# C of all head pairs from unsplit float32 weights, in 64x32 array tiles, in a packed attention and two-MLP kernel

## The chip, the cores and the metric

The kernel runs on one core of a Trainium2 chip. The metric is the device time of one execution in microseconds (us); less is better. The engines are PE (TensorE, matrix products), DVE (VectorE), ACT (ScalarE) and POOL (GpSimd); SP is the queue that starts transfers. The trace also shows the clock that PE was granted, 1.00 for 2.4 GHz and 0.50 for 1.2 GHz.

## The reference

q, k and v have the shape [8 batches, 8 heads, 576, 64], p has [8, 8, 32, 64]; all is float32, and the weights arrive as float64.

```python
scale = 1.0 / np.sqrt(q.shape[-1])
def sm_attn(qq, kk, vv):
    s = scale * np.matmul(qq, kk.transpose(0, 1, 3, 2))
    a = np.exp(s - np.max(s, axis=-1, keepdims=True))
    return np.matmul(a / (np.sum(a, axis=-1, keepdims=True) + 1e-09), vv)
p_packed = sm_attn(p, k, v)                # 32 packed keys per head
out = sm_attn(q, p_packed, p_packed)       # [8, 8, 576, 64]
x = out.transpose(0, 2, 1, 3).reshape(4608, 512)
g = x @ w_gate                             # [512, 1536]
x = g * (1 / (1 + np.exp(-g))) * (x @ w_val) @ w_out
out = ((x @ w1) * (x @ w2)) @ w3 @ w_out2  # second MLP
```

## The kernel before

**Order of the work.** A prologue (to about 119 us), written out by hand as a schedule of half steps, makes P = p_packed for 16 units, one for each batch b and half Q of the heads (four heads of 32 packed keys, so P is 128 x 64). `pa_P` (L545) scales P, `pa_PT` (L565) transposes it on PE. The attention of the queries ends in aT, the 32 weights of each query for each head. Instead of multiplying aT by P and the result by w_gate and w_val, the kernel first makes C = P·W, which has only 32 rows for each head, and then aT·C. This is exact algebra: `c_mm` makes C, `stage1` (L676) multiplies by aT and applies the gate, `stage3` (L701) multiplies by w_out.

**The 48 steps.** The batches go in four pairs P (P = 0 to 3 in the loop `for n, (P, f) in enumerate(steps)`, L878), and the 1536 gate and value columns in 12 blocks f of 128 + 128. A step makes C of the next step, `stage1` of both batches of the pair, and half of the `stage3` of three earlier blocks. The steps fill 119 to 870 us. The second MLP (L975 on) fills the rest.

**Precision.** A product of two float32 numbers is made as three float32r matmuls of halves, high·high, high·low and low·high. The halves come from `split`: ACT rounds to the high half, DVE or POOL subtracts. A plain float32 matmul is exact without splitting; the trace shows two records for each.

**C before.** For pairs 1 to 3, `w_load` fetches W's block into a `vl` buffer with tag "wf", `w_split` halves it (ACT: wh, L92; POOL: wl, L88), and `c_mm` takes twelve 128x128 matmuls of 256 columns. The weights are PTh and PTl, the halves of P transposed, laid out so that two heads and both batches of a pair fill the 128 columns, with zeros (from `mask`) where a head meets the other's rows. Pair 0 uses `c_first`: eight float32 matmuls, 128 rows by 64 columns, two side by side, from W as it was converted. `c_out` moves C out of PSUM as halves ch (ACT) and cl (DVE), in one operation each for pair 0 and in three each for the others. `q_mm` (scores of the queries) takes PT, the sum of PTh and PTl (L161), with four 128x32 array tiles side by side.

**Names and queues.** pc is C in PSUM; psq and psp are scores of the queries and of p; pg and pv are the gate and the value product; px is stage3's; acc is its sum over blocks. The PSUM pool of the steps, `ps`, has four buffers of two banks. In the prologue and in the second MLP the order on each engine is the code's; in the steps between, a scheduler orders the instructions of ACT, DVE, POOL and SP. During pair 1, 16 pieces of w1 and w2 are converted (`w12_conv`): a load raw_w, a shift vx_w (DVE, L345), ACT's w12t (L342), two DVE operations (L352, L355) and a store w12d.

Of the kernel before, what the change touches and what calls it, by code (L numbers as in the profile page):

```python
# [38 lines left out]
def packed_attention_moe_kernel(  # L39
# [112 lines left out]
    def q_T(b, Q):  # L152
        t = q_t.pop((b, Q))
        qT = qp.tile([128, 2, S], F32, tag="qT", name=f"qT{b}_{Q}")
        for pr in range(2):
            nc.vector.transpose(out=qT[:, pr], in_=t[:, pr].rearrange("p n d -> p (n d)"))
        PT = qp.tile([128, 128], F32, tag="PT", name=f"PT{b}_{Q}")
        for e in range(2):
            cols = slice(64 * ((b + e) % 2), 64 * ((b + e) % 2) + 64)
            hi, lo = (x[:, 2 * Q + e, b // 2 - 1, cols].bitcast(F32) for x in (PTh, PTl))  # L160
            nc.vector.tensor_tensor(out=PT[:, 64 * e:64 * e + 64], in0=hi, in1=lo, op=ALU.add)  # L161
        qT_t[b, Q] = (qT, PT)

    PTd_t = {}
# [18 lines left out]
    def q_rmm(b, Q):  # L183
        qT, PTd = qT_t.pop((b, Q)), PTd_t.pop((b, Q))
        if Q == 0:
            sT_t[b] = qp.tile([128, 2, 2, HS], F32, tag="sT", name=f"sT{b}")
        t = psum(f"psq{b}_{Q}")
        for at in range(4):
            hq = (at + 2 * (b % 2)) % 4
            for e in range(2):  # L190
# [1 line left out]
                nc.tensor.matmul(
                    t[32 * at:32 * at + 32, e, 0:HS].rearrange("j (m p) -> j m p", m=NR // 2),
                    lhsT=PTd[es, hs[hq]], rhs=qT[es, :, hs[hq]],
                    start=True, stop=True, tile_position=(64 * e, 32 * at))
# [221 lines left out]
    def c_first(f):  # L417
        w = wf_t.pop((0, f))
        t = psum(f"pc0_{f}").rearrange("p b (q n) -> p b q n", q=2)
        for b in range(2):  # L420
            for Q in range(2):
                for e in (b, 1 - b):
                    at = 64 * (e ^ b)
# [4 lines left out]
        return t  # L428

    def c_mm(P, f):  # L430
        if P == 0:
            t = c_first(f)
            if C_t.get("later"):
                return C_t["later"].append((P, f, t))
            return c_out(P, f, t)
        wh, wl = W_t.pop((P, f))
        t = psum(f"pc{P}_{f}").rearrange("p a (k n) -> p (a k) n", k=2)
        for kt in range(4):
            for x, (a, w) in enumerate(((PTh, wh), (PTh, wl), (PTl, wh))):
                nc.tensor.matmul(t[:, kt], lhsT=a[:, kt, P - 1, :], rhs=w[:, kt],  # L440
                                 start=(x == 0), stop=(x == 2))
        c_out(P, f, t)

    def c_out(P, f, t):
        hi = cp.tile([128, 2, 2, 256], F32R, tag="ch", name=f"ch{P}_{f}")
# [1 line left out]
        if P == 0:
            nc.scalar.copy(hi, t)
            sub(lo, t, hi)
            C_t[P, f] = (hi, lo)  # L450
            return
        tv = t.rearrange("p (q e) n -> p e q n", e=2)
        nc.scalar.copy(hi[0:64], tv[0:64])
        for e in range(2):
            nc.scalar.copy(hi[64:128, 1 - e], tv[64:128, e])  # L455
        sub(lo[0:64], tv[0:64], hi[0:64])
        for e in range(2):
            sub(lo[64:128, 1 - e], tv[64:128, e], hi[64:128, 1 - e])
# [85 lines left out]
    def pa_P(u):  # L544
# [13 lines left out]
        P_t[u] = Pz
        if u < 4:
            Pd = pa.tile([128, 2, 64], F32, tag="Pd", name=f"Pd{u}")  # L560
            for e in range(2):
                nc.vector.tensor_scalar(Pd[:, e], t[:, 0:64], sm, None, op0=ALU.mult)
            Pd_t[u] = Pd

    def pa_PT(u):  # L565
        b, Q = divmod(u, 2)
        Pz = P_t.pop(u)
        tb = psum1(f"pPT{u}")
        t = tb[:, 0:128]
        nc.tensor.transpose(t, Pz.rearrange("p a b -> p (a b)"), ident)  # L570
        if u < 4:
            nc.tensor.transpose(tb[:, 128:256], Pd_t.pop(u).rearrange("p a b -> p (a b)"), ident)
            PTd = pa.tile([128, 128], F32, tag="PTd", name=f"PTd{u}", bufs=4)
            nc.scalar.copy(PTd, tb[:, 128:256])
            PTd_t[b, Q] = PTd
            nc.scalar.copy(PT0[:, 2 * Q:2 * Q + 2, b], t.rearrange("p (e j) -> p e j", e=2))
            return
        at = [(2 * Q + e, b // 2 - 1, slice(64 * ((b + e) % 2), 64 * ((b + e) % 2) + 64)) for e in range(2)]
        for e in range(2):
            nc.scalar.copy(PTh[(slice(0, 128),) + at[e]], t[:, 64 * e:64 * e + 64])  # L580
        for e in range(2):
            sub(PTl[(slice(0, 128),) + at[e]], t[:, 64 * e:64 * e + 64], PTh[(slice(0, 128),) + at[e]])
# [529 lines left out]
```

## Time and profile before

| | us |
|---|---|
| median of three runs | 1445.25 (1442.3 to 1448.73) |
| the profiled execution | 1441.93, its span 1440.2 |
| PE busy | 1393.1 (97%) |
| DVE busy | 780.2 (54%) |
| ACT busy | 642.5 (45%) |
| POOL busy | 457.7 (32%) |
| mean granted clock of PE | 0.983 |

The span is what lies between the first and the last instruction of the profiled execution. Busy times are sums over the span. PE's records overlap, since matmuls are pipelined, so the distance between starts is what counts there.

### The profile page before, as it was taken

What the parts mean: (1) busy time and instruction counts of PE and PEld (TensorE: products, weight loads), DVE (VectorE), ACT (ScalarE), POOL (GpSimd) and SP (SyncE); (2) the same over time, 40 slices, a digit from 0 to 9 for tenths busy, and PEclk for the clock granted to TensorE, in tenths of its full rate; (3) what the DMA queues carried; (4) which work ended last, traced back from release to release, by engine and by line L of the source; (5) the groups of instructions that cost most, each with busy time, mean ns of one, the idle gap of its engine ahead of it and who ended that gap; (6) DMA issues with size and microseconds to landing.
All of it is one profiled execution on the core that took longest, in us unless ns stands there. A gap on an engine that the chain in (4) does not pass through costs nothing. (4 is left out here: it accounts for less than half of the span.)

```text
span 1440.2 us, 25384 instructions
## 1 busy us (share of the span) xinstructions
PE 1393.1 (97%) x9960; PEld 1302.1 (90%) x9960; DVE 780.2 (54%) x1188; ACT 642.5 (45%) x1077; POOL 457.7 (32%) x341
## 2 busy tenths in 40 slices
PE   7679999999999999999999999999999999999998
PEld 5457998999999999999989999989989899899997
DVE  3467798767875455756366647962333413334130
ACT  5575545536655355564464433643323323233231
POOL 0334133434544434455243223721202112021120
PEclk9888999999999999999999999999999999999999
DMA  9997575676533322215353324964827548275451
GB/s 270 239 248 205 163 210 188 160 237 166 165 83 83 117 60 70 66 53 176 96 157 100 131 72 174 339 242 154 256 75 236 179 133 253 92 223 180 133 168 44
DMA packets 175255, 230.26 MB, mean 160 GB/s; under 512 B 69408, under 2 KB 102176, under 8 KB 175136
## 3 DMA queue, kind: packets, MB, share of 16 engines
q1 hardware_dynamic: 175136, 228.64, 52.2%
q8 instruction: 79, 1.29, 0.4%
q14 instruction: 40, 0.33, 0.1%
HBM read 179.04 MB, written 49.55 MB: 159 GB/s over the span
## 5 line engine op out<-in xcount | busy, mean ns | idle before, releaser
L88 POOL TENSOR_TENSOR ul<-u,uh 128x576 fp32r<-128x576 f32 x96 | 145.4, 1519 | 247.7 <-ACT uh L92 247.3
L1005 POOL TENSOR_TENSOR c<-s,s 128x384 f32<-128x384 f32 x48 | 48.8, 1016 | 376.0 <-ACT s L1000 375.6
L701 PE MATMUL px<-ul,woh 128*128 128x288 f32 x768 | 165.3, 297 | 1.3 <-POOL ul L88 1.3
L701 PE MATMUL px<-uh,woh 128*128 128x288 f32 x768 | 165.4, 297 | 0.7 <-ACT uh L92 0.7
L701 PE MATMUL px<-uh,wol 128*128 128x288 f32 x768 | 164.9, 296 | 0.0
L1000 ACT COPY s<-pA 128x384 f32<-128x384 f32 x144 | 69.0, 479 | 181.1 <-PE pA L985 181.1
L88 DVE TENSOR_TENSOR cl<-pc,ch 64x512 fp32r<-64x512 f32 (+2 forms) x120 | 105.1, 900 | 55.4 <-ACT ch L455 47.6
L701 PEld LDWEIGHTS px<-uh,woh 128*128 128x128 f32 x768 | 124.1, 189 | 2.4 <-issue 1.4
L701 PEld LDWEIGHTS px<-ul,woh 128*128 128x128 f32 x768 | 124.3, 190 | 1.5 <-POOL ul L88 1.5
L701 PEld LDWEIGHTS px<-uh,wol 128*128 128x128 f32 x768 | 124.3, 189 | 0.0
L88 POOL TENSOR_TENSOR wl<-wf,wh 128x1024 fp32r<-128x1024 f32 x36 | 86.9, 2414 | 97.4 <-ACT wh L92 86.7
L1049 PE MATMUL po<-wo_hi,abl 128*128 128x512 f32 x288 | 112.2, 389 | 0.0
L1049 PE MATMUL po<-wo_lo,abh 128*128 128x512 f32 x288 | 112.1, 389 | 0.0
L1049 PE MATMUL po<-wo_hi,abh 128*128 128x512 f32 x288 | 112.0, 389 | 0.0
L711 DVE TENSOR_TENSOR acc<-acc,px 128x576 f32<-128x576 f32 x96 | 71.2, 746 | 66.1 <-PE px L701 65.9
L92 ACT CAST uh<-u 128x576 fp32r<-128x576 f32 x96 | 64.6, 674 | 93.5 <-DVE u L683 93.1
L88 DVE TENSOR_TENSOR abl<-ab,abh 128x768 fp32r<-128x768 f32 x48 | 48.6, 1013 | 105.2 <-ACT abh L92 105.2
L683 DVE TENSOR_TENSOR u<-u,pv 128x576 f32<-128x576 f32 x96 | 72.1, 751 | 48.8 <-PE pv L676 43.2
L88 POOL TENSOR_TENSOR wol<-wof,woh 128x512 fp32r<-128x512 f32 x48 | 66.9, 1406 | 88.3 <-ACT woh L92 80.7
L676 PE MATMUL pg<-aTh,ch 128*128 128x288 f32 x384 | 85.2, 304 | 4.8 <-DVE acc L711 3.3
L681 ACT ACTIVATE u<-pg 128x576 f32<-128x576 f32 x96 | 62.5, 651 | 49.4 <-PE pg L676 46.6
L676 PE MATMUL pg<-aTl,ch 128*128 128x288 f32 x384 | 83.3, 299 | 0.0
(362 smaller groups left out, 3544.1 us busy)
## 6 DMA issues: line engine op xcount, KB each, us to landing
ws<-wsd SPq DMA_DIRECT2D x245, 256.0 KB, 3.1
wf<-Wd SPq DMA_DIRECT2D x36, 512.0 KB, 3.4
raw_w<-in_moe_w_dram SPq DMA_DIRECT2D x32, 512.0 KB, 4.5
wsd<-ws SPq DMA_DIRECT2D x49, 256.0 KB, 4.0
raw_wo<-in_moe_w_out_dram SPq DMA_DIRECT2D x20, 512.0 KB, 4.4
km<-in_k_dram SPq DMA_DIRECT2D x16, 576.0 KB, 8.0
vm<-in_v_dram SPq DMA_DIRECT2D x16, 576.0 KB, 8.0
wof<-wod SPq DMA_DIRECT2D x36, 256.0 KB, 2.8
```

The lines of the kernel that those rows point to most:

```text
L88: eng.tensor_tensor(out=out, in0=src, in1=hi.bitcast(F32), op=ALU.subtract)
L92: nc.scalar.copy(hi, src)
L676: nc.tensor.matmul(t[:, hf, 0:HS], lhsT=w[:, b % 2, Q, cols], rhs=x[:, Q, hf, :], start=first, stop=last,)
L681: nc.scalar.activation(u, t[:, :, 0:HS], AF.Silu)
L683: nc.vector.tensor_tensor(out=u, in0=u, in1=t[:, :, 0:HS], op=ALU.mult)
L701: nc.tensor.matmul(t[:, hf, 0:HS], lhsT=w[:, 128 * d:128 * d + 128], rhs=x[:, hf, :], start=first, stop=last,)
L711: nc.vector.tensor_tensor(out=o, in0=o, in1=t[:, :, 0:HS], op=ALU.add)
L1000: nc.scalar.copy(o, t)
L1005: on.tensor_tensor(out=r, in0=o, in1=t, op=op)
L1049: nc.tensor.matmul(t, lhsT=a[:, j, cols], rhs=w[:, f], start=first, stop=last)
```

## The change

P is kept once, transposed, as PTd [128, 16 units, 128] in float32, doubled over the two halves of the partitions. C of all pairs is made by one `c_mm` from W as float32: sixteen matmuls, each with one head of one batch (64 rows) against its 256 columns, into 32 columns of the array; eight such tiles (two row halves by four column quarters) stand side by side. `w_split`, `c_first`, the masked Pz, PTh, PTl and PT0 go; `c_out` is one ACT and one DVE operation for all pairs. The order of the heads becomes `at ^ (b % 2)`. `q_mm` and `q_rmm` read PTd, with 64x32 tiles. `w_load` now fills the `wgv` buffers (tags "wh" and "wl" in turn, four in all) that held the halves.

```diff
-    PTh = pt_pool.tile([128, 4, NPR - 1, 128], F32R, name="PTh")
-    PTl = pt_pool.tile([128, 4, NPR - 1, 128], F32R, name="PTl")
-    PT0 = pt_pool.tile([128, 4, 2, 64], F32, name="PT0")
-    mask = const.tile([128, 2, 64], F32, name="mask")
+    PTd = pt_pool.tile([128, 2 * B, 128], F32, name="PTd")
...
+    def head(b, at):
+        return at ^ (b % 2)
...
     def q_mm(b, Q):
...
         for hf in range(2):
             for at in range(4):
-                hq = (at + 2 * (b % 2)) % 4
+                hq = head(b, at)
+                es = slice(64 * (hq % 2), 64 * (hq % 2) + 64)
                 nc.tensor.matmul(
-                    t[32 * at:32 * at + 32, hf, 0:HS],
-                    lhsT=PT[:, 32 * hq:32 * hq + 32],
-                    rhs=qT[:, hq // 2, HS * hf:HS * hf + HS],
-                    start=True, stop=True, tile_position=(0, 32 * at),
+                    t[hs[at], hf, 0:HS],
+                    lhsT=PTd[es, 2 * b + Q, hs[hq]],
+                    rhs=qT[es, hq // 2, HS * hf:HS * hf + HS],
+                    start=True, stop=True, tile_position=(64 * (hq % 2), 32 * at),
                 )
...
     def w_load(P, f):
-        t = vl.tile([128, 4, 2, 128], F32, tag="wf", name=f"wf{P}_{f}")
+        t = wgv.tile([128, 4, 2, 128], F32, tag=("wh", "wl")[f % 2], name=f"wf{P}_{f}")
...
+    def c_mm(P, f):
+        w = wf_t.pop((P, f))
+        t = psum(f"pc{P}_{f}").rearrange("p b (q n) -> p b q n", q=2)
+        for Q in range(2):
+            for at in range(4):
+                for b in range(2):
+                    hq = head(b, at)
+                    es = slice(64 * (hq % 2), 64 * (hq % 2) + 64)
                     nc.tensor.matmul(
-                        t[at:at + 64, b, Q], lhsT=PT0[:, 2 * Q + e, b],
-                        rhs=w[:, 2 * Q + e].rearrange("p g n -> p (g n)"),
-                        start=True, stop=True, tile_position=(0, at))
+                        t[hs[at], b, Q], lhsT=PTd[es, 2 * (2 * P + b) + Q, hs[hq]],
+                        rhs=w[es, 2 * Q + hq // 2].rearrange("p g n -> p (g n)"),
+                        start=True, stop=True, tile_position=(64 * (hq % 2), 32 * at))
...
-        Pz = pa.tile([128, 2, 64], F32, tag="Pz", name=f"Pz{u}")
-        for e in range(2):
-            nc.vector.scalar_tensor_tensor(
-                Pz[:, e], t[:, 0:64], sm, mask[:, e], op0=ALU.mult, op1=ALU.mult)
+        Pd = pa.tile([128, 2, 64], F32, tag="Pd", name=f"Pd{u}")
+        nc.vector.tensor_scalar(
+            Pd, t[:, 0:64].rearrange("p (o d) -> p o d", o=1).to_broadcast([128, 2, 64]), sm, None, op0=ALU.mult)
...
+        t = psum1(f"pPT{u}")[:, 0:128]
+        nc.tensor.transpose(t, Pd_t.pop(u).rearrange("p a b -> p (a b)"), ident)
+        nc.scalar.copy(PTd[:, u], t)
...
-        if at(2) is not None and at(2)[0] > 0:
-            w_split(*at(2))
```

PE's order keeps its places, but for the form of C and three steps of pair 3. This is PE in pair 1, where C of block 1 (pc_1) stands between the px of the step before and pg of block 0. Before:

```order
L440 MATMUL pc_1_3587<-wh_1_3470,PTh 128x256 [waits DVE_49]
L440 MATMUL pc_1_3587<-wl_1_3471,PTh 128x256 [waits Pool_49]
L440 MATMUL pc_1_3587<-wh_1_3470,PTl 128x256
L440 MATMUL pc_1_3587<-wh_1_3470,PTh 128x256
...
L440 MATMUL pc_1_3587<-wh_1_3470,PTl 128x256
L676 MATMUL pg_0_3609<-aTh_2759,ch_0_3491 128x288 [waits DVE_49]
```

And after the change:

```order
L617 MATMUL pv_11_3543<-aTh_1249,ch_11_3381 128x288 x2
L617 MATMUL pv_11_3543<-aTl_1250,ch_11_3381 128x288 x2
L617 MATMUL pv_11_3543<-aTh_1249,cl_11_3382 128x288 x2
L408 MATMUL pc_1_3575<-wf_1_3418,PTd 32x256 [waits DMAHW3_49,DVE_49]
L408 MATMUL pc_1_3575<-wf_1_3418,PTd 32x256 x15
L617 MATMUL pg_0_3597<-aTh_2733,ch_0_3487 128x288 [waits DVE_49]
```

Twelve instructions become sixteen smaller ones, and the waits for the halves of W (among them POOL's) give way to a wait for the transfer of wf itself.

On SP, in pair 1, the loads wf_4 and wf_5 stand among the pieces of q (qr), the loads of w1 and w2 (raw_w), the stores w12d and those of the finished sums (X2d<-acc). Before:

```order
L382 DMA wf_4_3926<-Wd 128x1024 [waits DMAHW3_49,Pool_49]
L145 DMA qr_1_3978<-in_q_dram 32x18x32 [waits DMAHW4_49]
L145 DMA qr_1_3978<-in_q_dram 32x18x32 [waits DMAHW5_49]
L145 DMA qr_1_3978<-in_q_dram 32x18x32 [waits DMAHW6_49]
L382 DMA wf_5_4049<-Wd 128x1024 [waits DMAHW7_49,Pool_49]
L713 DMA X2d<-acc_0_2144 128x576 [waits DMAHW0_49,DVE_49]
L324 DMA raw_w_5_4092<-in_moe_w_dram 128x512 [waits DMAHW1_49]
L713 DMA X2d<-acc_1_2165 128x576 [waits DMAHW2_49,DVE_49]
L720 DMA w12d<-w12t_4086 128x4x128 [waits DMAHW3_49]
```

After:

```order
L372 DMA wf_4_3910<-Wd 128x1024 [waits PE_49]
L138 DMA qr_1_3959<-in_q_dram 32x18x32 [waits DMAHW1_49]
...
L372 DMA wf_5_4026<-Wd 128x1024 [waits DMAHW7_49,PE_49]
L314 DMA raw_w_5_4069<-in_moe_w_dram 128x512 [waits DMAHW0_49]
L654 DMA X2d<-acc_0_2094 128x576 [waits DMAHW1_49,DVE_49]
L661 DMA w12d<-w12t_4063 128x4x128 [waits DMAHW2_49]
L654 DMA X2d<-acc_1_2115 128x576 [waits DMAHW3_49,DVE_49]
```

The loads wait for PE in place of POOL, wf_4 stands ahead of more pieces of q, and raw_w_5 and the store behind it have each moved ahead of a store of acc.

On DVE, a little later in pair 1, the subtraction cl_2 stands near the shift of raw_w_10. Before:

```order
L355 SCALAR_TENSOR_TENSOR w12t_4612<-raw_w_5_4092,vx_w_5_4613 128x512 [waits DMAHW6_49,DVE_49]
...
L355 SCALAR_TENSOR_TENSOR w12t_5152<-raw_w_8_4618,vx_w_8_5153 128x512 [waits DMAHW7_49,DVE_49]
L88 TENSOR_TENSOR cl_2_3886<-pc_2_3872,ch_2_3885 64x1024 [waits PE_49,Activation_49]
L88 TENSOR_TENSOR cl_2_3886<-pc_2_3872,ch_2_3885 64x512 x2
L683 TENSOR_TENSOR u_1_3893<-u_1_3893,pv_1_3908 128x576 [waits PE_49,Activation_49]
L345 TENSOR_SCALAR vx_w_10_5545<-raw_w_10_5032 128x512 [waits DMAHW4_49,DVE_49]
```

After:

```order
L345 SCALAR_TENSOR_TENSOR w12t_5096<-raw_w_8_4580,vx_w_8_5097 128x512 [waits DMAHW7_49,DVE_49]
L335 TENSOR_SCALAR vx_w_10_5481<-raw_w_10_4983 128x512 [waits DMAHW0_49,DVE_49]
L88 TENSOR_TENSOR cl_2_3874<-pc_2_3856,ch_2_3873 128x1024 [waits Activation_49]
L624 TENSOR_TENSOR u_1_3877<-u_1_3877,pv_1_3892 128x576 [waits PE_49,Activation_49]
L342 SCALAR_TENSOR_TENSOR vx_w_9_5296<-w12t_5295,vx_w_9_5296 128x512 [waits Activation_49]
```

The shift of raw_w_10, which waits for its load, now stands ahead of cl_2 and of the u behind it.

## Rows read from the trace of the kernel before

**Rows 1.** The page, parts 1 and 5: busy time and share; a group of POOL.

```profile
PE 1393.1 (97%) x9960; PEld 1302.1 (90%) x9960; DVE 780.2 (54%) x1188; ACT 642.5 (45%) x1077; POOL 457.7 (32%) x341
...
L88 POOL TENSOR_TENSOR wl<-wf,wh 128x1024 fp32r<-128x1024 f32 x36 | 86.9, 2414 | 97.4 <-ACT wh L92 86.7
```

**Rows 2.** Stretches: length, busy time (count) of each engine, granted clock, DMA share, GB/s.

```profile
core 0: us, PE busy (x) PEld busy (x) DVE busy (x) ACT busy (x) POOL busy (x), PEclk, DMA share, GB/s
102.00:112.20 10.20, 8.91 (x90) 5.83 (x94) 6.00 (x21) 6.41 (x16) 4.27 (x3) 0.50 0.69 198
...
180.00:216.00 36.00, 36.00 (x273) 34.03 (x273) 35.37 (x49) 16.75 (x27) 13.74 (x8) 1.00 0.77 210
216.00:252.00 36.00, 36.00 (x288) 31.55 (x288) 29.17 (x40) 19.13 (x26) 13.66 (x9) 1.00 0.60 188
...
317.10:323.80 6.70, 6.10 (x25) 6.10 (x26) 5.19 (x8) 3.46 (x6) 3.63 (x2) 0.50 0.76 245
...
450.00:680.00 230.00, 230.00 (x1774) 226.59 (x1773) 128.13 (x166) 120.05 (x174) 111.20 (x69) 1.00 0.31 93
```

**Rows 3.** C's matmuls by form: duration ns min/median/max, first and last start.

```profile
L424 PE MATMUL pc<-wf,PT x192: 379/379/690, 106.8 to 267.5; 128*64 128x256 f32 x192
...
L440 PE MATMUL pc<-wh,PTh x144: 277/283/395, 274.3 to 852.7; 128*128 128x256 f32 x144
```

**Rows 4.** Timeline of PE, pair 0: start, us, what, count of records.

```profile
236.67 0.43 PE L676 MATMUL pv<-aTh,cl 128*128 128x288 f32 x2
237.03 1.18 PE L208 MATMUL psq<-qT,PT 128*32 128x288 f32 x16
238.13 1.95 PE L424 MATMUL pc<-wf,PT 128*64 128x256 f32 x16
240.01 0.53 PE L676 MATMUL pg<-aTh,ch 128*128 128x288 f32 x2
240.38 0.43 PE L676 MATMUL pg<-aTl,ch 128*128 128x288 f32 x2
240.65 0.30 PE L676 MATMUL pg<-aTh,cl 128*128 128x288 f32 x1
```

**Rows 5.** Timeline of PE, pair 1, a step without psq.

```profile
309.55 0.28 PE L440 MATMUL pc<-wh,PTh 128*128 128x256 f32 x1
...
310.99 0.43 PE L676 MATMUL pg<-aTh,ch 128*128 128x288 f32 x2
```

**Rows 6.** Timeline of PE, pair 1, a step behind psq.

```profile
413.03 0.39 PE L440 MATMUL pc<-wh,PTh 128*128 128x256 f32 x1
...
414.57 0.43 PE L676 MATMUL pg<-aTh,ch 128*128 128x288 f32 x2
```

**Rows 7.** Timeline of PE in the prologue, around a psp.

```profile
91.77 0.72 PE L514 MATMUL psp<-kT 64*32 64x288 f32 x16
92.42 0.33 PE L570 MATMUL pPT<-ident,Pz 128*128 128x128 f32 x1
```

**Rows 8.** Timeline of PE, the prologue's last C, transpose and the first pg.

```profile
106.83 3.68 PE L424 MATMUL pc<-wf,PT 128*64 128x256 f32 x16
110.45 1.52 PE L537 MATMUL pat<-ident,ap 128*96 128x128 f32 x6
...
117.69 0.30 PE L570 MATMUL pPT<-ident,Pz 128*128 128x128 f32 x1 [1.10 <-DVE Pz L556]
119.42 0.82 PE L676 MATMUL pg<-aTh,ch 128*128 128x288 f32 x2 [1.43 <-DVE cl L88]
```

**Rows 9.** Timelines of PE, DVE and ACT, the stall at 314 us.

```profile
317.70 0.85 PE L676 MATMUL pg<-aTh,ch 128*128 128x288 f32 x2 [3.35 <-DVE acc L711]
...
313.20 0.69 DVE L352 SCALAR_TENSOR_TENSOR vx_w<-w12t,vx_w 128x512 int32<-128x512 int32 x1 [2.40 <-ACT w12t L342]
...
312.50 0.66 ACT L342 ACTIVATE w12t<-raw_w 128x512 f32<-128x512 f32 x1 [5.79 <-DMA w12d<-w12t]
```

**Rows 10.** Timeline of SP's queue: start and length of each issue.

```profile
283.97 0.34 SPq L382 DMA_DIRECT2D wf<-Wd  x1
...
290.68 0.34 SPq L382 DMA_DIRECT2D wf<-Wd  x1
```

More of the change, by code (lines that the diff above doesn't have):

```diff
@@ L109, in packed_attention_moe_kernel @@
     pt_pool = pool("pt", "right")
-    PTh = pt_pool.tile([128, 4, NPR - 1, 128], F32R, name="PTh")
-    PTl = pt_pool.tile([128, 4, NPR - 1, 128], F32R, name="PTl")
-    PT0 = pt_pool.tile([128, 4, 2, 64], F32, name="PT0")
-    mask = const.tile([128, 2, 64], F32, name="mask")
-    nc.vector.memset(mask, 0.0)
-    for hq in range(4):
-        nc.vector.memset(mask[32 * hq:32 * hq + 32, hq % 2, :], 1.0)
+    PTd = pt_pool.tile([128, 2 * B, 128], F32, name="PTd")
     vl = pool("vl", "left", bufs=2)
@@ L156, in q_T @@
             nc.vector.transpose(out=qT[:, pr], in_=t[:, pr].rearrange("p n d -> p (n d)"))
-        PT = qp.tile([128, 128], F32, tag="PT", name=f"PT{b}_{Q}")
-        for e in range(2):
[L159 to L164, printed above, removed]
+        qT_t[b, Q] = qT
+    def head(b, at):
+        return at ^ (b % 2)
     def q_rows(b, Q):
@@ L183, in q_rmm @@
     def q_rmm(b, Q):
-        qT, PTd = qT_t.pop((b, Q)), PTd_t.pop((b, Q))
+        qT = qT_t.pop((b, Q))
         if Q == 0:
@@ L193, in q_rmm @@
                     t[32 * at:32 * at + 32, e, 0:HS].rearrange("j (m p) -> j m p", m=NR // 2),
[L194 removed]
+                    lhsT=PTd[es, 2 * b + Q, hs[hq]], rhs=qT[es, :, hs[hq]],
                     start=True, stop=True, tile_position=(64 * e, 32 * at))
@@ L199, in q_mm @@
     def q_mm(b, Q):
-        qT, PT = qT_t.pop((b, Q))
+        qT = qT_t.pop((b, Q))
         if Q == 0:
@@ L366, in conv @@
             raw_load()
-    W_t, wf_t, wst_t = {}, {}, {}
+    wf_t, wst_t = {}, {}
     def w_conv(f, gv):
@@ L415, in wo_split @@
         wo_t[P, f] = (hi, lo)
[L417 to L423, printed above, removed]
-                    nc.tensor.matmul(
-                        t[at:at + 64, b, Q], lhsT=PT0[:, 2 * Q + e, b],
-                        rhs=w[:, 2 * Q + e].rearrange("p g n -> p (g n)"),
-                        start=True, stop=True, tile_position=(0, at))
[L428 to L441, printed above, removed]
+    def c_mm(P, f):
[4 more added lines that the diff above has]
+                for b in range(2):
+                    hq = head(b, at)
+                    es = slice(64 * (hq % 2), 64 * (hq % 2) + 64)
+                    nc.tensor.matmul(
+                        t[hs[at], b, Q], lhsT=PTd[es, 2 * (2 * P + b) + Q, hs[hq]],
+                        rhs=w[es, 2 * Q + hq // 2].rearrange("p g n -> p (g n)"),
+                        start=True, stop=True, tile_position=(64 * (hq % 2), 32 * at))
+        if C_t.get("later"):
+            return C_t["later"].append((P, f, t))
         c_out(P, f, t)
@@ L446, in c_out @@
         lo = cp.tile([128, 2, 2, 256], F32R, tag="cl", name=f"cl{P}_{f}")
[L447 to L458, printed above, removed]
+        nc.scalar.copy(hi, t)
+        sub(lo, t, hi)
         C_t[P, f] = (hi, lo)
@@ L486, in load_kv @@
         kv[nm, u] = m
-    kT_t, ap_t, apT_t, sm_t, P_t, Pd_t = {}, {}, {}, {}, {}, {}
+    kT_t, ap_t, apT_t, sm_t, Pd_t = {}, {}, {}, {}, {}
     def pa_kT(u):
@@ L553, in pa_P @@
                     start=(r == 0), stop=(r == NV - 1), tile_position=(0, 32 * hq))
-        Pz = pa.tile([128, 2, 64], F32, tag="Pz", name=f"Pz{u}")
-        for e in range(2):
-            nc.vector.scalar_tensor_tensor(
-                Pz[:, e], t[:, 0:64], sm, mask[:, e], op0=ALU.mult, op1=ALU.mult)
[L558 to L563, printed above, removed]
-    def pa_PT(u):
[L566 to L582, printed above, removed]
+        Pd = pa.tile([128, 2, 64], F32, tag="Pd", name=f"Pd{u}")
+        nc.vector.tensor_scalar(
+            Pd, t[:, 0:64].rearrange("p (o d) -> p o d", o=1).to_broadcast([128, 2, 64]), sm, None, op0=ALU.mult)
+        Pd_t[u] = Pd
+    def pa_PT(u):
+        t = psum1(f"pPT{u}")[:, 0:128]
+        nc.tensor.transpose(t, Pd_t.pop(u).rearrange("p a b -> p (a b)"), ident)
+        nc.scalar.copy(PTd[:, u], t)
     U = 2 * B
```

7 lines of the change are left out of this document (removed).

## The prediction

> **What bounds the kernel now.** I read the page's first part, then a table of stretches, then PE's own rows. PE is busy for 97% of the span, DVE for 54% [rows 1]. The table of stretches [rows 2] says where that average hides something: in 450–680 us PE has no idle time at all, and the time is PE's instructions one after another. Three places differ. In 102–112 us, the end of the prologue, PE waits and runs at a granted clock of 0.50. In 180–216 us DVE is busy 35.37 of 36 us beside a full PE. At 317–324 us PE runs at half clock behind a stall of 3.35 us [rows 9]. So a microsecond taken out of PE's stream in the 48 steps is a microsecond of the end, unless DVE cannot follow; work taken off ACT and POOL is worth nothing by itself. POOL stands idle 97.4 us ahead of the very subtractions that go (2414 ns each) [rows 1].
>
> **The forms of C's matmuls.** What matters of a matmul is the distance from its start to the next one's, not the 379 or 283 ns of its record [rows 3], since they overlap.
>
> *Pair 0 now.* A psq (four tiles side by side, so 4 rounds of 288 columns: 16 records, two per fp32 matmul) lasts 238.13 − 237.03 = 1.10 us; the c_first behind it (two side by side, 8 rounds of 256) 240.01 − 238.13 = 1.88 [rows 4]. Two equations, 1152c + k = 1.10 and 2048c + k = 1.88, give c = 0.87 ns a column, 0.223 us for a round of 256, and k = 0.10.
>
> *Pairs 1 to 3 now.* Twelve matmuls, 310.99 − 309.55 = 1.44 us, 0.12 each, with nothing lost at either side [rows 5].
>
> *After.* Sixteen matmuls of 256 columns, eight side by side: 4 rounds. The nearest row is psp, also 64x32 tiles, eight at once, 2 rounds of 288: 92.42 − 91.77 = 0.65 [rows 7]; 576c is 0.50, so its k is 0.15. The new C lasts 4 × 0.223 + 0.10 to 0.15 = 0.99 to 1.04. I take 1.04, psp's constant.
>
> *Going in and out of small tiles.* Ahead of psq, the last pair of pv takes 237.03 − 236.67 = 0.36, where a pair takes 240.65 − 240.38 = 0.27 otherwise; behind c_first the first pair of pg takes 0.37 [rows 4]. That is 0.09 in and 0.10 out. Pair 0 pays this now and afterwards; pairs 1 to 3 begin to pay it. The Trainium skill, TensorEngine Tiling (Array Packing), Key Properties, says that changing the tiling mode drains the array. These rows agree, at 0.19 us for both ways; the page gives no price.
>
> **The sum, in microseconds off the profiled execution.**
>
> 1. *Pair 0*: ten of its twelve C steps lie among the 48 steps (c_first's 192 records [rows 3] are 16 each; two are in the prologue). 1.88 − 1.04 = 0.84 each: 8.4. Bounds 0.84 to 0.89.
> 2. *Pairs 1 to 3*: 36 steps. By the code, a psq stands right ahead of the c_mm after f = 2, 7 and 8 in pairs 1 and 2, so six steps are already in small tiles when C begins. Such a step now costs 414.57 − 413.03 = 1.54 [rows 6] and then 1.04 + 0.10: 0.40 saved, 2.4 for six. Three steps of pair 3 are cut in two by the matmuls of w3·w_out2 (3 and 9 before, 1 and 15 afterwards): they switch twice more for 0.19 + 0.19, and 0.2 either way each comes out as nothing. The other 27 go from 1.44 to 1.04 + 0.19 = 1.23: 0.21 each, 5.7. Together 8.1. With 1.15 or 1.33 for the whole of it (the tiles' k as psq's 0.10 and a little less for the switch; or the switch half as dear again) it is 5 to 10.5.
> 3. *DVE in pair 0*: a step is 24 pairs of stage1 and, on the mean, 24 of stage3 at 0.27, and C: some 14.8 us. So 180–216 us holds two and a half, and PE would need 2.1 us less there. DVE has 0.63 us to spare [rows 2], and gives up only its additions for PT, some tenths. The other stretches have room (29.17 of 36 in 216–252). PSUM has four buffers, and a pg that waits for a late DVE stops everything queued behind it on PE. I give back 1.0 of item 1; bounds 0 to 4.
> 4. *The prologue's tail*: PE stands 1.10 us for Pz and 1.43 for cl before the first pg; the first C takes 110.45 − 106.83 = 3.6 at half clock [rows 8] and would take about 2. Two masked products become one broadcast product, two subtractions for PTl go, one transpose of two goes. But the tail also hangs on the prologue's loads, which stay. Of 1.6 + about 1 for the shorter DVE chain I take 2.0; bounds 0 to 3.5.
> 5. *The stall at 314 us*: PE waits 3.35 us for an acc, which stands behind a conversion on DVE, which waits for ACT's w12t, and that waited 5.79 us for a store of w12d [rows 9]. The store's queue, SP, sits in front of wf_4 until 283.97 and of wf_5 until 290.68 [rows 10], because their buffers come free only with POOL's splitting. In the new order both loads wait for a c_mm of four steps earlier, long done, raw_w_5 follows one place sooner, and the chain gets some 2 us ahead. But cl_2 now stands behind the shift of raw_w_10 on DVE, a row later than before. The idle time could fall by the 2 us or move; I take 1.5. If idle and half clock both vanish it is 3.35 + half of 6.7 = 6.7 [rows 2, 9]; if cl_2 becomes the late one, −2.
> 6. *Nothing*: the halving of wh (ACT), wl (POOL), the six-part c_out, PTh and PTl. They are on engines that PE does not wait for over most of the steps; the cover is PE's own 14 us a step. The transfer of wf stays as large, and lands well ahead. c_out as one copy and one subtraction per step shortens only the distance to the stage1 a step later. The second MLP is the same code: 0.
>
> 8.4 + 8.1 − 1.0 + 2.0 + 1.5 = 19.0; 1441.9 − 19.0 = 1422.9. The profiled execution is 3.3 us below the median of its runs (1445.25), so on the scale of the median I forecast 1426.
>
> **Rivals.**
>
> - *More is gained*: the stall at 314 us and its half clock go away as a whole (5 us more than item 5), and the rest as forecast: 1421, or 1418 with the best end of item 2. For it: the chain starts earlier. Against it: the stall is made by a store that ACT waits 5.79 us for [rows 9], and the stores remain. 0.10.
> - *Half is given back*: DVE, in pair 0, takes 4 us back (item 3), the switch costs more (item 2 is 5), the tail yields 0 as its loads set the time, and the stall only moves: 8.4 − 4 + 5 = 9.4, so 1436. For it: DVE at 35.37 of 36 [rows 2]; against it: the stretches beside it have 6 us of slack. 0.17.
> - *Slower: the row halves do not overlap.* In psp each row half of the array writes a PSUM bank of its own. In the new C both row halves write one bank at one time, at different quarters of the partitions, and in q_mm likewise. No row of before shows that. If such writes take turns, C has 8 rounds: 1.78 + 0.15 + 0.19 = 2.12 against 1.44, +0.68 on some 33 steps, +22; item 1 is nothing; q_mm becomes 8 rounds in place of 4, +0.9 on 12 calls, +11. With 2 for the tail and 1.5 for the stall: +30, so 1475. It decides from the point where C with its switches lasts over 1.44. Against it: within each quarter of the partitions the two row halves are on different banks, as in psp. 0.07. The Trainium skill, TensorEngine Tiling (Array Packing), Gotcha 1: PSUM Pressure, says that different row tiles cannot access the same PSUM bank at the same time. Taken literally this would be the rival; no row of before shows the case either way.
> - *Anything else slower*: a new late load or DVE conversion of the size of the one at 314 us in each of several steps, as the scheduler's order moved. 0.03.
>
> **How the numbers follow.** Forecast 0.63 (1418 to 1432), more 0.10, half 0.17, slower 0.10. A change of under 0.5% (7.2 us) is about what cannot be told from none: faster is below 1438.0. The forecast, the larger gain and a little less than half of the half case (its bounds of 1432 to 1442) lie below it: 0.80. The rest of the half case, and 0.01 of the slower ones, is same: 0.11; slower 0.09. For the range I take 1417 to 1438: the bounds of items 1, 2 and 5 downwards, the half case upwards; it leaves out the slower cases, the far end of the half case and of the larger gain.
>
> **What would show it.** In the trace of the changed kernel: pc in pair 0 and in pair 2 from its first start to the following pg, 1.0 to 1.1 us after a psq, with the pair of px or pv ahead of it stretched to about 0.36; 1.44 or more in pair 2 would turn item 2 over, about 1.9 would be the bank rival. In 180–216 us or its counterpart, idle of PE with DVE as releaser tells item 3. The first pg at about 117.4 us tells item 4, and PE's idle time near 312 us and the clock there item 5. From the pair 3 steps on, the two kernels should run at a constant distance; if the second MLP's length moved, the prediction left something out.

## The result, and the profile after

The changed kernel takes 1430.71 us (median, 1430.03 to 1435.5), the kernel before beside it 1446.99; the ratio is 0.9896 with a 95% interval of 0.9858 to 0.9934. A second comparison in five rounds (below) gave 1431.99 against 1445.25, ratio 0.9912, 0.9889 to 0.9935. The forecast was 1426 in a range of 1417 to 1438. The profiled execution lasted 1431.37 us, its span 1429.6: 10.6 us less than before's, where the sum said 19.0.

The page's first part for the changed kernel, which answers to the first line of [rows 1]:

```profile
PE 1372.7 (96%) x10868; PEld 1259.5 (88%) x10868; DVE 705.2 (49%) x1039; ACT 569.1 (40%) x953; POOL 367.2 (26%) x305
```

And stretches, with the columns of [rows 2]; the first line is the kernel before, the others the changed kernel:

```profile
144.00:180.00 36.00, 36.00 (x287) 32.49 (x286) 27.37 (x42) 19.41 (x28) 7.15 (x6) 1.00 0.58 163
...
144.00:180.00 36.00, 33.44 (x276) 31.20 (x275) 25.69 (x38) 18.65 (x28) 7.51 (x5) 1.00 0.58 160
180.00:216.00 36.00, 32.53 (x281) 30.02 (x282) 35.48 (x49) 17.44 (x28) 11.90 (x8) 1.00 0.71 207
...
450.00:680.00 230.00, 230.00 (x2134) 215.89 (x2117) 108.57 (x134) 89.53 (x129) 74.31 (x53) 1.00 0.31 94
```

POOL lost 90 us of work and ACT 73, and PE is still full in 450–680 us. What is new stands in 144–216 us: PE idles 2.56 + 3.47 = 6.0 us there, where before it had no idle time, and DVE is as full in 180–216 us (35.48 of 36) as before.

The form of C, in PE's timeline of pair 0 (first two rows) and pair 2 (the others), as in [rows 4, 5]:

```profile
134.19 1.09 PE L408 MATMUL pc<-wf,PTd 64*32 64x256 f32 x32
135.21 0.53 PE L617 MATMUL pg<-aTh,ch 128*128 128x288 f32 x2
...
441.38 0.43 PE L642 MATMUL px<-uh,wol 128*128 128x288 f32 x2
441.74 1.09 PE L408 MATMUL pc<-wf,PTd 64*32 64x256 f32 x32
442.76 0.53 PE L617 MATMUL pg<-aTh,ch 128*128 128x288 f32 x2
443.13 0.42 PE L617 MATMUL pg<-aTl,ch 128*128 128x288 f32 x2
```

From its first start to pg it lasts 1.02 us in both (1.04 forecast). The pair of px ahead of it takes 0.36 and the first pg behind it 0.37: 0.09 in and 0.10 out, as read before.

The next table cuts each trace at starts on PE: the first pg, then the 25th (pair 1 begins; 96 in all), the 33rd, the 79th (in pair 3), the 95th, and the first pA of the second MLP. All runs are told of below; "again" is the changed kernel's second profile. The times are us between the two starts.

| run | first pg at | pair 0: 1st to 25th pg | four steps: to 33rd | 23 steps: to 79th | eight steps: to 95th | to the first pA | first pg to first pA |
|---|---|---|---|---|---|---|---|
| before | 119.4 | 164.5 | 78.8 | 322.7 | 174.0 | 29.6 | 769.6 |
| after | 118.5 | 162.5 | 75.4 | 316.2 | 174.4 | 31.5 | 760.0 |
| after, again | 118.5 | 162.5 | 76.6 | 316.2 | 176.2 | 30.0 | 761.4 |
| e1 old head order | 116.3 | 168.3 | 78.0 | 335.9 | 180.2 | 31.5 | 794.0 |
| e2 halving kept | 116.7 | 166.1 | 79.6 | 319.9 | 180.3 | 30.0 | 775.9 |
| e3 old load buffers | 113.2 | 162.0 | 80.2 | 315.9 | 174.5 | 31.5 | 764.1 |
| e4 softmax to POOL | 117.7 | 171.4 | 76.6 | 322.3 | 174.6 | 28.9 | 773.9 |
| e5 X prepared later | 121.7 | 162.5 | 77.3 | 315.9 | 176.1 | 28.5 | 760.2 |
| e8 before, no halving | 119.3 | 164.1 | 80.4 | 322.7 | 175.6 | 29.6 | 772.4 |
| e9 aT later | 118.0 | 162.7 | 76.8 | 315.9 | 174.4 | 31.5 | 761.3 |
| e11 no sign in pair 0 | 118.4 | 158.1 | 76.5 | 315.9 | 174.6 | 30.4 | 755.5 |
| e13 sign to ACT and POOL | 115.5 | 168.0 | 77.2 | 315.9 | 174.5 | 28.9 | 764.5 |
| e12 X prepared later | 111.8 | 163.4 | 77.7 | 315.9 | 174.4 | 28.5 | 759.8 |
| e14 with low w_out on DVE | 116.5 | 166.1 | 76.6 | 315.9 | 176.2 | 28.5 | 763.2 |

The second MLP itself, from the first to the 145th of its 150 runs of pA, is 501.9 to 503.2 us in all of them. Where the eight steps take 176 us and not 174.4, it is the clock: in e5 PE was granted 0.92 in 745–760 us, in the changed kernel's first profile 1.00. So the 23 steps, the long stretch on PE alone, gave what the sum said, the eight steps of pair 3 gave nothing, and pair 0, with the largest term of the sum, gave 2.1 us.

### The profile page after: what moved, and what is told of

Read it like the earlier page. It is cut to its first block, busy times and chain, and to the rows that moved or that the text cites. A ratio compares the mean times of both kernels' runs of the same rounds, so it can differ in the third digit from the quotient of the medians.

```text
span 1429.6 us, 26827 instructions
## 1 busy us (share of the span) xinstructions
PE 1372.7 (96%) x10868; PEld 1259.5 (88%) x10868; DVE 705.2 (49%) x1039; ACT 569.1 (40%) x953; POOL 367.2 (26%) x305
## 3 DMA queue, kind: packets, MB, share of 16 engines
q8 instruction: 86, 1.41, 0.4%
## 4 chain that ended last, share of the span: by engine, by line
PE 85%; DMA 6%; DVE 5%; ACT 2%; issue 1%; POOL 1%; SPq 0%; DVEq 0%; ACTq 0%; POOLq 0%
PE px L642 20%; PE pA L924 14%; PE po L988 14%; PE pg L617 9%; PE pv L617 8%; PE pB L924 7%; PE pC L924 3%; PE pc L408 3%; DMA km<-in_k_dram 2%; DMA raw_w<-in_moe_w_val_dram 2%; PE pk L460 1%; DMA w12d<-w12t 1%; DVE u L624 1%; DMA qr<-in_q_dram 1%; PE psq L198 1%
## 5 line engine op out<-in xcount | busy, mean ns | idle before, releaser
L88 POOL TENSOR_TENSOR wol<-wof,woh 128x512 fp32r<-128x512 f32 x48 | 63.4, 1334 | 130.1 <-ACT woh L92 130.1
L617 PE MATMUL pg<-aTh,ch 128*128 128x288 f32 x384 | 88.3, 311 | 3.5 <-DVE u L624 1.9
L617 PE MATMUL pv<-aTh,ch 128*128 128x288 f32 x384 | 83.2, 298 | 4.3 <-ACT u L622 2.2
L617 PE MATMUL pg<-aTh,cl 128*128 128x288 f32 x384 | 82.8, 297 | 0.0
```

The lines of the kernel that those rows point to most:

```text
L88: eng.tensor_tensor(out=out, in0=src, in1=hi.bitcast(F32), op=ALU.subtract)
L617: nc.tensor.matmul(t[:, hf, 0:HS], lhsT=w[:, b % 2, Q, cols], rhs=x[:, Q, hf, :], start=first, stop=last,)
```

## The experiments

**e1, the head order of before.** What does C owe to eight tiles side by side?

```diff
     def head(b, at):
-        return at ^ (b % 2)
+        return (at + 2 * (b % 2)) % 4
```

> The changed kernel with the head order of before (C's tiles of both batches of a pair then fall on the same row half and column quarter, so four tiles side by side and not eight). Theory 1, the gain is C's four rounds in place of eight: C lasts 8 x 0.223 + 0.10 = 1.9 us in place of 1.02, 36 steps of pairs 1 to 3 lose 0.86 each, six of them another 0.2 since psq and C no longer overlap; pair 0 loses 8.6 but wins back the 5.9 us that PE idles there. About +35 on the profiled 1431.4: 1466. Rival, the gain is from work taken off ACT, POOL and SP: the time stays within 5 us of 1431.

Measured: 1463.6 us, before beside it 1440.41. C in e1's PE timeline:

```profile
132.89 1.97 PE L408 MATMUL pc<-wf,PTd 64*32 64x256 f32 x32
134.79 0.54 PE L617 MATMUL pg<-aTh,ch 128*128 128x288 f32 x2
```

It lasts 1.90 us with the same 16 instructions: eight rounds, as c_first's 1.88. The rival is out: with all of the lighter ACT, POOL and SP the kernel is 23 us slower than before. This is 119–216 us of e1, and its longest wait on PE there:

```profile
119.00:216.00 97.00, 94.99 (x816) 86.77 (x815) 80.58 (x110) 49.24 (x74) 30.94 (x20) 0.99 0.70 193
...
195.89 0.54 PE L642 MATMUL px<-uh,woh 128*128 128x288 f32 x2 [1.61 <-DVE u L624]
```

PE's idle time is 97.00 − 94.99 = 2.0 us here and 6.0 in the changed kernel, with the same work on DVE; the trace has the instructions of DVE, ACT and POOL in the changed kernel's order. So 4.0 us of that wait come from PE's being faster. The other 2.0 stand here though C is as long as before, and most of them are one wait.

**e2, the halving kept, and e3, the loads in their old buffers without it.** Is work off ACT and POOL worth nothing?

```diff
     def w_load(P, f):
-        t = wgv.tile([128, 4, 2, 128], F32, tag=("wh", "wl")[f % 2], name=f"wf{P}_{f}")
+        t = vl.tile([128, 4, 2, 128], F32, tag="wf", name=f"wf{P}_{f}")
...
+    def w_split(P, f):                                         # from here on e2 alone
+        hi = wgv.tile([128, 4, 256], F32R, tag="wh", name=f"wh{P}_{f}")
+        lo = wgv.tile([128, 4, 256], F32R, tag="wl", name=f"wl{P}_{f}")
+        split(hi, lo, wf_t[P, f].rearrange("p k g n -> p k (g n)"), sub_on="pool")
...
+        if at(2) is not None and at(2)[0] > 0:
+            w_split(*at(2))
```

> The changed kernel with the loads of W in their old buffers and the halving of W by ACT and POOL kept, its halves unread. Theory 1: PE's form alone makes the gain, so only the stall near 314 us comes back, 2 us: 1432 to 1435. Rival, ACT and POOL off the chain make the gain of pairs 1 to 3 (7 us without the stall): most of that is lost, 1437 to 1441, with new idle time of PE in pairs 1 to 3.

> The changed kernel with W loaded into its old buffers, and no halving. Theory 1, the halves' work on ACT and POOL is what held the run with the halving kept: none of its stalls near 239 to 248, 650 and 745 us is there, and from the first pg to the second MLP the time is within 2 us of the changed kernel's (759.9 us). Rival, the place of the buffer and the queue in front of it: those stalls are there, 765 to 775 us from the first pg to the second MLP.

Measured: e2 1445.71 us, 5 over the kernel before beside it (1440.41); e3 1431.25 against 1443.62. The halves in e2 are made and not read. Against the changed kernel e2 loses 3.6 us in pair 0, where the first halves of pair 1 are made, 4.2 in the four steps, 3.7 in the 23 steps and 6 in pair 3; there PE was also granted 0.77 in 745–760 us. This is the wait at 651.71 us of e2, on PE, with DVE and POOL ahead of it:

```profile
651.71 0.53 PE L622 MATMUL pg<-aTh,ch 128*128 128x288 f32 x2 [1.74 <-DVE acc L657]
...
646.21 2.95 DVE L335 TENSOR_SCALAR vx_w<-raw_w 128x512 int32<-128x512 int32 x2
649.09 1.90 DVE L342 SCALAR_TENSOR_TENSOR vx_w<-vt_w,vx_w 128x512 int32<-128x512 int32 x1
650.91 0.74 DVE L657 TENSOR_TENSOR acc<-acc,px 128x576 f32<-128x576 f32 x1
...
646.25 2.63 POOL L88 TENSOR_TENSOR wl<-wf,wh 128x1024 fp32r<-128x1024 f32 x1 [1.78 <-issue]
```

The halving (wl, 2.63 us on POOL) and DVE's shifts of raw_w lie side by side, the two shifts take 2.95 us (0.41 and 2.62) where one takes 0.43 by itself, and acc is late. e3, with the same buffers and no halving, has none of these waits, so they belong to the halving and not to the place of the buffer. That holds for 319.9 against 315.9 us in the 23 steps and, but for the clock, for 180.3 against 174.5 in pair 3. e3's own loss is in the first four steps of pair 1 (80.2 against 75.4 to 77.7 in the nine others with C in eight tiles and no halving). Its loads of wf leave as early as the changed kernel's, but the scheduler ordered DVE otherwise between 260 and 380 us, and PE waits for a cl behind a shift that waits for its load:

```profile
309.79 0.52 PE L617 MATMUL pv<-aTh,ch 128*128 128x288 f32 x2 [2.76 <-DVE cl L88]
...
308.18 0.43 DVE L335 TENSOR_SCALAR vx_w<-raw_w 128x512 int32<-128x512 int32 x1 [2.18 <-DMA raw_w<-in_moe_w_dram]
308.52 1.22 DVE L88 TENSOR_TENSOR cl<-pc,ch 128x1024 fp32r<-128x1024 f32 x1
```

**e8, the kernel before without the halving.** The other half of that question.

```diff
-        t = vl.tile([128, 4, 2, 128], F32, tag="wf", name=f"wf{P}_{f}")
-        nc.sync.dma_start(t, Wd[f])
-        wf_t[P, f] = t
+        t = wgv.tile([128, 4, 256], F32R, tag=("wh", "wl")[f % 2], name=f"wf{P}_{f}")
+        nc.sync.dma_start(t.bitcast(F32), Wd[f].rearrange("p k g n -> p k (g n)"))
+        W_t[P, f] = (t, t)
...
-            w_split(*at(2))
```

> The kernel before with W's halving left out (the twelve matmuls of C take W unsplit as both halves, so C of pairs 1 to 3 is wrong; PE's work is the same) and W loaded into the buffers of the halves. Theory 1, work off ACT and POOL pays only where PE waits: PE idles in before only near 314 us (with the half clock 6.7 us lost) and in pair 3 (some 4 us), so the time from the first pg to the second MLP falls from 769.6 by 2 to 7 us. Rival, it is worth 14 us by itself, as the run with the halving kept lost: 754 to 757 us. Second rival, nothing: 769 to 771 us.

Measured: 1445.36 us against 1443.62; 772.4 us from the first pg to the second MLP, nothing gained (2.8 us more than before, 1.6 of them in pair 3, where PE ran at half clock for 3.4 us). The second rival stands. So lighter ACT and POOL alone give nothing, the shorter C with the halving kept gives nothing (e2, 775.9), and both together give 760.0. The relief pays only once PE is faster. At the wait of e2 shown above the reason is DVE, stretched beside POOL and late; that it is the same at e2's other waits is not shown.

**e4, three softmax operations of the queries on POOL.** Pair 0's loss: DVE's load?

```diff
-            3: lambda: (q_mm(b, 1), q_max(b), q_sub(b)),
+            3: lambda: (q_mm(b, 1), q_max(b), q_sub(b, on="pool")),
-            5: lambda: (q_sum(b), q_div(b)),
-            6: lambda: (q_aT(b, 0), q_aT(b, 1)),
+            5: lambda: (q_sum(b), q_div(b, on="pool")),
+            6: lambda: (q_aT(b, 0, "pool"), q_aT(b, 1, "pool")),
```

> The changed kernel with three of the queries' softmax operations of the 48 steps (subtract the maximum, divide, low half of aT) moved from DVE to POOL. Theory 1, pair 0 lost its gain because DVE's load as a whole is the bound there: PE's idle time between 119 and 216 us falls from 5.9 to under 3 us, 1427 to 1429. Rival, DVE's operations last two to three times as long while POOL works (1.1 to 1.8 against 0.68 us in the changed kernel's pair 0), so more work on POOL slows DVE as much as it relieves it: idle time 5 us or more, 1430 to 1434.

Measured: 1445.08 us against 1440.41, and pair 0 takes 171.4 us, 9 more. PE ran at half clock for 10.2 us of it, against 3.4 in the changed kernel, so some 3.4 of the 9 us are the clock's (an estimate, half of the difference). Its worst wait, on PE, with DVE and POOL beside each other:

```profile
183.05 0.53 PE L617 MATMUL pv<-aTh,ch 128*128 128x288 f32 x2 [4.23 <-DVE cl L88]
...
177.82 2.50 DVE L345 SCALAR_TENSOR_TENSOR wf<-raw_w,vx_w 128x512 int32<-128x512 int32 x1
180.24 0.68 DVE L342 SCALAR_TENSOR_TENSOR vx_w<-wf,vx_w 128x512 int32<-128x512 int32 x1
...
177.38 2.38 POOL L241 TENSOR_TENSOR sT<-sT,qsm 128x1152 f32<-128x1152 f32 x1 [2.33 <-DVE qsm L237]
```

The conversion on DVE takes 2.50 us and ends 0.56 after POOL's operation, where the next one takes 0.68. The rival is right in its direction and too mild in its size. The experiment doesn't tell whether DVE's load is the bound, since it didn't lower it: DVE is busy for 134 to 135 us of pair 0 in both kernels, here with seven operations fewer.

**e9, one aT a step later.**

```diff
-            6: lambda: (q_aT(b, 0), q_aT(b, 1)),
+            6: lambda: (q_aT(b, 0), at and q_aT(b, 1)),
+            7: lambda: at or q_aT(b, 1),
```

> The changed kernel with one of the two transposes of the queries' weights (aT of the second half of the heads, first batch of a pair, with its halving) written one step later, so that DVE's crowded stretch near 180 to 216 us gets 1.5 to 2.6 us less. Theory 1, the pile of DVE's work there takes pair 0's gain: PE's idle time in 119 to 216 us falls from 6.0 to under 4 us, and the time from the first pg to the first pg of pair 1 from 162.4 to under 161. Rival, the pile only moves: 162 or more.

Measured: 1432.93 us against 1443.62, pair 0 162.7 us. Neither theory: the scheduler put DVE's instructions in exactly the order of the changed kernel, so the edit moved nothing. The run stands as a repeat, and shows how far one profile is to be trusted: 0.2 us in pair 0, 1.4 in the four steps behind it.

**e11, the operation for the sign left out in pair 0, and e13, that operation on ACT and POOL.**

```diff
+            bare = dve and key.startswith(("w_", "wo_"))       # e11
             nc.vector.scalar_tensor_tensor(
-                x, t.bitcast(I32), 3, x, op0=ALU.logical_shift_left, op1=ALU.bitwise_or)
-            if dve:
+                t.bitcast(I32) if bare else x, t.bitcast(I32), 3, x, op0=ALU.logical_shift_left, op1=ALU.bitwise_or)
+            if bare:
+                pass
+            elif dve:
...
-DSIGN = ('w',)
+DSIGN = ('w1', 'w3', 'wo2')                                    # e13
```

> The changed kernel with one of DVE's three operations for each converted piece of w_gate, w_val and w_out left out in the 48 steps (the one that sets the sign, so those weights lose their sign; everything else is done): 28 operations of 0.68 us or more, all in pair 0. Theory 1, DVE's load in pair 0 is what PE waits for: PE's idle time in 119 to 216 us falls from 6.0 to under 2.5 us, and the time from the first pg to the first pg of pair 1 from 162.5 to under 159. Rival, the waits hang on buffers or loads: 161.5 or more.

> The changed kernel with those 28 operations of DVE done on ACT (the sign) and POOL (the product with it), everything computed. Theory 1 in its strong form, only the count of DVE's own operations matters: like the run without the sign, the time from the first pg to the first pg of pair 1 under 159. Rival, POOL's operations stretch DVE's that run beside them (those without PSUM, 1.1 to 1.8 in place of 0.68 us), so 28 more of POOL take back what was won: 161 or more.

Measured: e11 1427.19 us, e13 1433.37, before beside them 1441.38. The stretch 119–216 us, in e11, in e13 and in the changed kernel:

```profile
119.00:216.00 97.00, 94.81 (x845) 88.45 (x844) 67.16 (x90) 51.51 (x78) 31.26 (x22) 0.97 0.72 211
```
```profile
119.00:216.00 97.00, 88.64 (x800) 81.26 (x800) 73.43 (x87) 60.88 (x95) 59.15 (x42) 1.00 0.65 188
```
```profile
119.00:216.00 97.00, 90.97 (x812) 83.72 (x812) 80.56 (x110) 50.48 (x76) 31.06 (x21) 0.98 0.69 195
```

With DVE at 67 of 97 us in place of 81, PE's idle time falls from 6.0 to 2.2 us and pair 0 to 158.1 us: DVE's load is the cause of 3.8 of the 6.0 us. With the same operations on ACT and POOL, DVE's remaining ones take longer (73.4 us), PE idles 8.4, and pair 0 takes 168.0. The rival of e13 stands.

**e5 and e12, X prepared a step later; e14, that and the low half of w_out on DVE in pair 0; e15, the changed kernel again.** e5 and e12 are the same program; e5 is one run, e12 four, e14 and e15 six each.

```diff
             if f == 10:
                 x2_prep(0, 1)
+            if f == 11:
                 x2_prep(0, 2)
-            if f == 11:
                 x2_prep(0, 3)
...
-        split(hi, lo, wof_t.pop((P, f)), sub_on="pool")
+        split(hi, lo, wof_t.pop((P, f)), sub_on="pool" if P else "dve")     # e14 only
```

> The changed kernel with one part of the preparation of X for the second MLP (T4, halves of T2 and B22) written one step later, behind the last stage1. Theory 1: the last u of DVE stands behind these halves, which makes PE wait for uh 1.23 and ul 1.55 us at 855 to 858 us; the waits fall under 1 us together and the distance of the two kernels at the first matmul of the second MLP grows from 10.55 to 12 or more: 1428 to 1430. Rival: the waits move to the start of the second MLP, 1431 to 1433.

> The changed kernel with the part of X's preparation (T4, halves of T2 and B22) one step later, five times against the kernel before. By the first trace of it, 3 us from the last stage1 to the second MLP (28.5 in place of 31.5 us), the rest unchanged: 2 to 3 us below the changed kernel. Rival: within 1 us of it.

> The same, and in pair 0 the low half of w_out is subtracted by DVE in place of POOL: 12 operations of some 0.65 us more on DVE, 12 of 1.4 us less on POOL. If DVE's load alone counts, pair 0 gets longer: 164 us or more from the first pg to the first pg of pair 1. If POOL's operations cost DVE as much as they take over, it stays at 162 to 163; if more, it falls under 161.5.

> The changed kernel again, five times against the kernel before on the same chip. If the change is worth what the stages of the traces say (9.6 us from the first pg to the second MLP, the prologue a coin toss of a few us either way), the ratio is 0.991 to 0.995; the forecast of 19 us would be 0.987.

Measured: e5 1434.53 against 1440.41, above both of its cases; its first pg came 3.2 us later than the changed kernel's, and one wait of 1.53 us remained. The others go against one median of before (1445.25): e15 1431.99, ratio 0.9912 (0.9889 to 0.9935), the first of its two cases, and the interval leaves out the 0.987 of 19 us; e12 1427.89, 0.9879 (0.9854 to 0.9904); e14 1432.75, 0.9914 (0.9886 to 0.9942). These are the waits at the end of pair 3 in the changed kernel, on PE, and DVE's order ahead of them:

```profile
856.31 0.53 PE L642 MATMUL px<-uh,woh 128*128 128x288 f32 x2 [1.23 <-ACT uh L92]
858.39 0.53 PE L642 MATMUL px<-ul,woh 128*128 128x288 f32 x2 [1.55 <-POOL ul L88]
...
850.97 2.18 DVE L88 TENSOR_TENSOR xB22l<-x2r,xB22h 128x768 fp32r<-128x768 f32 x1
853.07 0.95 DVE L768 TENSOR_TENSOR x2T<-x2r,x2T 128x768 f32<-128x768 f32 x1
853.94 0.95 DVE L88 TENSOR_TENSOR xT2l<-x2T,xT2h 128x768 fp32r<-128x768 f32 x1
854.81 1.41 DVE L624 TENSOR_TENSOR u<-u,pv 128x576 f32<-128x576 f32 x2
```

And in e12, one wait in place of two, with a u ahead of T4 (x2T) and the halves of T2:

```profile
853.08 0.53 PE L642 MATMUL px<-ul,woh 128*128 128x288 f32 x2 [1.52 <-POOL ul L88]
...
849.28 0.74 DVE L624 TENSOR_TENSOR u<-u,pv 128x576 f32<-128x576 f32 x1
849.95 0.95 DVE L768 TENSOR_TENSOR x2T<-x2r,x2T 128x768 f32<-128x768 f32 x1
```

In that stretch the three profiles with the later X take 28.5 us, where the changed kernel took 31.5 and 30.0. The order is worth 1.5 us of that: the first profile also ran at half clock for 3.4 us, from 859.3 on, and the second did not. e4 and e13, with X where it was, took 28.9, since they lack a wait that the changed kernel has at its first pA, 0.94 us for the last acc. e12 is the fastest of the versions that leave nothing out, 4.1 us below e15 by the medians; their intervals overlap, and only 1.5 us are told by the traces. e14 goes the way of the first of its three cases: 12 more operations on DVE cost pair 0 2.7 to 3.6 us.

## Why the prediction was right, and where its sum was off

**The form of C (items 1 and 2) was right, in mechanism and size.** 1.02 us against 1.04, in and out 0.19. Ten steps of pair 0 could give 0.86 each. The 23 steps between pair 1 and pair 3 give 322.7 − 316.2 = 6.5 us; 18 × 0.21 and 5 steps with psq at 0.58 (1.10 + 1.54 before, 1.96 + 0.10 now) make 6.7. A step with psq gives more than the 0.40 forecast, because psq and C run into each other (last section). The three cut steps of pair 3, priced at nothing, cost some 1.2 us together: the eight steps there are 0.4 us longer than before in the first profile, where their four plain ones alone would have saved 0.8.

**DVE in pair 0 (item 3) is the step that failed in size.** The mechanism stood in the prediction, at 1.0 us with a bound of 4. Ten C (8.6), three psq that run into C (0.5) and two C of pair 1 that fall in this stretch (0.4) could give about 9.5 us. Measured are 2.1, so 7.4 went back, more than the bound of 4. PE's idle time is 6.0 us of it, and a stop costs more than its idle time, as around the longest one:

```profile
195.59 0.42 PE L617 MATMUL pv<-aTh,cl 128*128 128x288 f32 x2
197.71 0.53 PE L642 MATMUL px<-uh,woh 128*128 128x288 f32 x2 [1.70 <-DVE u L624]
198.08 0.42 PE L642 MATMUL px<-ul,woh 128*128 128x288 f32 x2
```

Without the idle time the pair of pv takes 0.42 us and the pair of px 0.37, where a pair takes 0.27: 0.25 on top. Of the eight stops between 146 and 208 us, six lie where C's own going in and out doesn't cover this, so some 1.5 us. The prediction put the bound at the spare time of DVE in one stretch, 0.63 us, and asked by how much PE would outrun it. But PE also idles 2.56 us in 144–180, where DVE is busy for 25.69 of 36 us (27.37 before), as at 146.60 us:

```profile
146.60 0.53 PE L617 MATMUL pv<-aTh,ch 128*128 128x288 f32 x2 [0.96 <-DVE u L624]
...
142.94 1.41 DVE L342 SCALAR_TENSOR_TENSOR vx_w<-wf,vx_w 128x512 int32<-128x512 int32 x1 [1.01 <-ACT wf L332]
...
145.20 0.68 DVE L342 SCALAR_TENSOR_TENSOR vx_w<-wf,vx_w 128x512 int32<-128x512 int32 x1
145.81 0.74 DVE L624 TENSOR_TENSOR u<-u,pv 128x576 f32<-128x576 f32 x1
...
142.38 1.42 POOL L88 TENSOR_TENSOR ul<-u,uh 128x576 fp32r<-128x576 f32 x1 [3.41 <-ACT uh L92]
```

The u that frees a PSUM buffer stands behind four conversions in DVE's order, and the first of them waits 1.01 us for ACT and takes 1.41 beside POOL's ul. What counts here is how much DVE has queued ahead of one operation that PE needs, not its mean. e11 shows that the load is the cause of most of it, and e1 that PE's pace brings out 4.0 of the 6.0 us. The other 2.0 the prediction had nowhere: the wait at 197.71 us stands in e1 too, at the old pace of C, while in the kernel before, with DVE in another order, PE has no idle time in 180–216 us [rows 2]. The new order of the instructions beside PE is the likely cause; no run puts the old order back.

**The prologue's tail (item 4, 2.0 us)** can't be judged from a pair of profiles. The ten other profiles with the changed kernel's prologue (all but e1 and e8) reach their first pg between 111.8 and 121.7 us; before and e8 at 119.4 and 119.3, the changed kernel at 118.5.

**The stall at 314 us (item 5, 1.5 us)** went as the prediction's doubt had it: it moved. SP issues wf and raw_w early, as forecast from [rows 10]:

```profile
281.08 0.34 SPq L372 DMA_DIRECT2D wf<-Wd  x1
281.47 0.43 SPq L314 DMA_DIRECT2D raw_w<-in_moe_w_dram  x1
```

The wait of 3.35 us in [rows 9] is gone, but PE then waits in two later places, 3.5 us in all. Both hang on ACT's w12t, which waits for a store of w12d as in [rows 9]; the first through a conversion and a u on DVE, the second through the u behind it on ACT:

```profile
320.10 0.53 PE L617 MATMUL pg<-aTh,ch 128*128 128x288 f32 x2 [1.32 <-DVE u L624]
...
324.15 0.53 PE L617 MATMUL pv<-aTh,ch 128*128 128x288 f32 x2 [2.19 <-ACT u L622]
...
317.98 0.67 ACT L332 ACTIVATE w12t<-raw_w 128x512 f32<-128x512 f32 x1 [1.15 <-DMA w12d<-w12t]
322.90 0.67 ACT L332 ACTIVATE w12t<-raw_w 128x512 f32<-128x512 f32 x1 [1.23 <-DMA w12d<-w12t]
323.47 0.63 ACT L622 ACTIVATE u<-pg 128x576 f32<-128x576 f32 x1
...
318.69 0.69 DVE L342 SCALAR_TENSOR_TENSOR vx_w<-w12t,vx_w 128x512 int32<-128x512 int32 x1 [4.03 <-ACT w12t L332]
319.30 0.75 DVE L624 TENSOR_TENSOR u<-u,pv 128x576 f32<-128x576 f32 x1
```

The shift of raw_w_10 ahead of cl_2, which the prediction feared, cost nothing in this profile; the wait of e3 above is of that kind. The four steps gave 78.8 − 75.4 = 3.4 us, of which 1.2 are C's; in e5, e9, e12 and the repeat, with the same order there, they gave 1.1 to 2.2 in all. So this item is worth between nothing and 2.2 us. What it gave is the clock and not the wait: PE was at 0.50 for 6.7 us there before [rows 2] and at 1.00 in the changed kernel's first profile.

**The work taken off ACT and POOL (item 6, 0)** was right by itself (e8) and wrong as said: with it kept, the shorter C gains nothing (e2). And the handover to the second MLP, taken as the same code, lost 1.9 us in the first profile and 0.4 in the repeat, which alone of the three had no half clock there. Some 0.8 of it is the last u of stage1, which moved behind X's halves, and 0.9 the wait for acc at the first pA, which the kernel before doesn't have and whose cause stays open; e5 and e12 win 1.5 back by order alone.

**The rivals.** The row halves do overlap: C would have lasted 1.9 us, as it does in e1. The half-given-back case named the right mechanism, DVE in pair 0. The time of 1430.7 lies inside the forecast's own 1418 to 1432, near the end where that case begins. That it came so near is in part luck: the sum's 19.0 us are 10.6 between the two profiles, while the medians differ by 16.3 us in the first comparison and 13.3 in the second. From the first pg to the second MLP the traces show 9.6; where the rest of the medians' distance lies, none shows.

## What to carry to other kernels

When the engine that bounds a stretch gets faster, ask of the next engine what it has queued ahead of each operation that the first one needs, and not what its mean load in the stretch is; and look at what a new order of its instructions does by itself. Work taken off engines beside the path may be worth nothing alone and still be what lets the path get shorter, so undo the two parts one by one in both kernels. Side work moved from DVE to POOL can cost more than it frees, since POOL stretches DVE's conversions.
